# Turning three of four feature chunks by transposing transfers instead of TensorE

## The chip, the cores and the metric

The kernel runs on one core of one Trainium2 chip. The metric is the time of one execution in device microseconds (us), taken as the median of several runs. The engines named below are TensorE (PE: matrix products, with its weight loads listed as PEld), VectorE (DVE), ScalarE (ACT), GpSimd (POOL) and SyncE (SP), whose queue issues nearly all transfers of this kernel (SPq in the profile).

## The reference

The input x has 2048 rows (tokens) of 640 features. The output is x plus an attention block and an MLP block, both of which see x after two layer norms in a row (one outside, one within the MLP, or one for the attention).

```
xn = layernorm(x)
q, k, v = split(xn @ wqkv)                 # 32 heads of 20 features
o = softmax(q k^T / sqrt(20)) v            # per head, over all 2048 tokens
A = concat(o) @ wo
h = gelu(layernorm(xn) @ w1 + b1)          # 640 -> 1536
B = h @ w2 + b2                            # 1536 -> 640
out = x + A + B
```

The products are needed at about single precision. The kernel gets there with 16-bit operands: each number is written as a sum of a high and a low float16, and a product of two such sums is taken as three TensorE passes (high by high, high by low, low by high).

## The kernel before, in words

The kernel has two stages. The first, up to about 232 us, makes q, k and v of all tokens and prepares the weights of the MLP. The second holds the attention, with the MLP's products and the last projection woven between its scores; the change does not touch it. In the first stage a manual schedule is in force: each engine executes its instructions in the order in which the program text issues them, and the same holds for the queue of SP. A wait at the head of an engine's list holds up all that stands behind it.

The tokens are taken in four chunks c = 0 to 3 of 512. For each chunk, `load_x` (L169) brings four tiles `xt` of 128 rows by 640 features, of which five buffers exist. `norm_a`, `norm_b` and `norm_c` (L230 to L252) compute the layer norms on VectorE, scale the tiles in place, and store 512 numbers of 4 bytes each to `rscr` (L252). TensorE needs the features on the partitions. So `transp` (L262) turns the 20 blocks of 128x128 of a chunk on TensorE with an identity, in three groups of 8, 8 and 4 blocks, into PSUM, and `transp_out` copies them from there, with ScalarE for the high half (L269) and VectorE for the low half (L270), into the tile `xnt` of the chunk. After the last group the whole tile is also stored to `xscr` (L272) for the MLP.

The products of a chunk follow. `qk(c, tt)` for tt = 0 to 4 (L286) makes a pair of 128 columns of q or k for the 512 tokens, thirty products of 128x512. `qk_out` evicts it: ScalarE writes the high half (L300), VectorE the low half (L301), the squares for the heads' lengths follow (L304 on ScalarE in chunk 0, L306 on VectorE after it), and SP stores both halves to `qkscr` (L308, 256 KB each). `lengths()` (L321) is a small TensorE product on those squares; it stands after the next `qk` in TensorE's order, so TensorE waits there if the squares are late. Then `vproj(c, j)` for j = 0 to 3 (L349) makes the values and `vproj_out` evicts them (L359, L361). All these products, and before the change the turned blocks, share three buffers of PSUM (pool `psS`).

While chunk c is multiplied, chunk c + 1 is normalized and turned: its `transp` groups stand after tt = 2, 3 and 4 of chunk c. The x tiles of chunk c + 2 are requested after tt = 4.

Beside this runs the preparation of weights. In chunk 0 the weights of k and v are split (L382, L383), w2 (L474) and w1 (L482) are requested by SP, 3.8 MB each, and the generator `weights()` then yields slices of work which `some(n)` places: sums of squares of w2 (L415, six slices), a scale, sums of squares of w1 (L423, five slices), a scale, common factors, and the splitting of w2 and w1 into halves (L125 to L127). These run on ScalarE and VectorE between the evictions.

The row of constants is `brow`, 32 heads by 2048 float16. GpSimd fills it at the start (L446), the row of ones for k is stored to `bscr` (L458), and in the last chunk `shifts()` scales it per head (L340) and stores it (L341), from where the first scores' operands read it.

The instructions issued by SP wait, each, for the transfer issued eight before it, since eight semaphores are used in turn.

Of the kernel before, what the change touches and what calls it, by code (L numbers as in the profile page):

```python
# [8 lines left out]
F16 = mybir.dt.float16  # L9
BF16 = mybir.dt.bfloat16  # L10
I32 = mybir.dt.int32
AF = mybir.ActivationFunctionType
# [4 lines left out]
P = 128  # L17
S, D, H, DH, F = 2048, 640, 32, 20, 1536
KD = D // P
# [23 lines left out]
def mha_mlp_kernel(tc, x, wqkv, wo, w1, b1, w2, b2, out):  # L43
    nc = tc.nc
# [3 lines left out]
    with (  # L48
# [9 lines left out]
        xscr = dram.tile([P, KD, 2, S], F16, name="xscr")  # L58
# [6 lines left out]
        bscr = dram.tile([H + 1, S], F16, name="bscr")  # L65
# [12 lines left out]
        w1t = keep.tile([P, KD, F], F32, name="w1t")  # L78
# [76 lines left out]
        with tc.tile_pool(name="pa", bufs=2) as pa, tc.tile_pool(name="pa1", bufs=1) as pa1, tc.manual_schedule():  # L155
# [7 lines left out]
            xts = {}  # L163
# [31 lines left out]
            for m in range(KD):  # L195
# [3 lines left out]
                nc.gpsimd.affine_select(heads[:, m, :], heads[:, m, :], pattern=[[DH, H]],  # L199
                                        compare_op=ALU.is_ge, fill=0.0, base=DH - 1 - m * P,  # L200
                                        channel_multiplier=-1)
            brow = pa1.tile([H, S], F16, name="brow")
            lmx = pa1.tile([P, 2, 4], F32, name="lmx")

            def warm(n):
# [48 lines left out]
            xnts = {}  # L254

            def transp(c, k0, pts):
                if k0 == 0:
                    xnts[c] = pa.tile([P, KD, 2, 512], F16, tag="xnt", name=f"xnt{c}")
                pt = psS.tile([P, 2, 512], F32, tag="s", name="pt")
                for j in range(4):  # L260
                    for k in range(min(2, KD - k0)):
                        nc.tensor.transpose(pt[:, k, j * P : (j + 1) * P],  # L262
                                            xts[c][j][:, (k0 + k) * P : (k0 + k + 1) * P], ident)
                pts.append((c, k0, pt))

            def transp_out(c, k0, pt):
                nk = min(2, KD - k0)
                ks = slice(k0, k0 + nk)
                nc.scalar.activation(xnts[c][:, ks, 0, :], pt[:, :nk], AF.Copy)  # L269
                nc.vector.tensor_sub(xnts[c][:, ks, 1, :], pt[:, :nk], xnts[c][:, ks, 0, :])  # L270
                if k0 + 2 > KD:
                    nc.sync.dma_start(xscr[:, :, :, c * 512 : (c + 1) * 512], xnts[c])  # L272
                    del xts[c]

            PASS = ((0, 0), (0, 1), (1, 0))

            def qk(c, tt):
                ps = psS.tile([P, 2, 512], F32, tag="s", name="qkp")
                order = [(i, k) for i in range(2) for k in range(KD)]
                if c + tt == 0:  # L280

                    order = [(i, k) for k in range(KD) for i in range(2)]
                for i, k in order:
                    q, mm = divmod(2 * tt + i, KD)
                    for n, (a, b) in enumerate(PASS):
                        nc.tensor.matmul(ps[:, i, :], wv[:, k, q, a, mm * P : (mm + 1) * P],  # L286
                                         xnts[c][:, k, b, :], start=(k + n == 0), stop=(k == KD - 1 and n == 2))
                return ps
# [39 lines left out]
            def shifts():  # L328

                b = sm.tile([H, 2], F32, tag="b", name="b")  # L330
                bq = sm.tile([H, 2, 4], F32, tag="bq", name="bq")
                for r in range(4):
                    nc.vector.tensor_reduce(bq[:, :, r], lmx[32 * r : 32 * r + 32], AX.X, ALU.max)
                nc.vector.tensor_reduce(b, bq, AX.X, ALU.max)
                nc.vector.tensor_scalar(b[:, 0:1], b[:, 0:1], b[:, 1:2], 1e-30, ALU.mult, ALU.max)
                nc.gpsimd.tensor_tensor(b[:, 0:1], b[:, 0:1], half, ALU.pow)
                nc.vector.tensor_scalar(b[:, 0:1], b[:, 0:1], -1.01, TOP / QS, ALU.mult, ALU.add)
                nc.vector.tensor_scalar(b[:, 0:1], b[:, 0:1], 0.0, -65504.0 * KROW, ALU.min, ALU.max)
                nc.vector.tensor_scalar(b[:, 0:1], b[:, 0:1], 1.0 / KROW, 1.0 / KROW, ALU.mult, ALU.mult)
                nc.vector.tensor_scalar(brow, brow, b[:, 0:1], None, ALU.mult)  # L340
                nc.sync.dma_start(bscr[:H, :], brow)  # L341

            def vproj(c, j):
                ps = psS.tile([P, 2, 512], F32, tag="s", name="vp")
                for hf in range(2):
                    n = 0
                    for k in range(KD):
                        for a, b in PASS:
                            nc.tensor.matmul(ps[:, hf, :320], xnts[c][:, k, a, j * P : (j + 1) * P],  # L349
# [18 lines left out]
            def sums(tag, ws):  # L368
                accs[tag] = squares(ws, junk)
# [9 lines left out]
            def split_qkv(n):  # L379
                q = "qkv".index(n)  # L380
                for k in range(KD):
                    nc.scalar.activation(wv[:, k, q, 0], stage[n][:, k], AF.Copy, scale=scales[n])  # L382
                    nc.vector.scalar_tensor_tensor(wv[:, k, q, 1], stage[n][:, k], scales[n], wv[:, k, q, 0],  # L383
                                                   ALU.mult, ALU.subtract)
# [54 lines left out]
            def some(n):  # L439
                for _ in range(n):  # L440
                    next(slices, None)
# [7 lines left out]
            pts = []  # L449
# [5 lines left out]
            for t in pts:  # L455
                transp_out(*t)
            split_qkv("q")
            nc.sync.dma_start(bscr[H : H + 1, :], brow[0:1, :])  # L458
            nc.sync.dma_start(b1t, b1.rearrange("(k p) -> p k", p=P))
            for c in range(4):  # L460
                nxt = c + 1 if c < 3 else None
                for tt in range(5):
                    ps = qk(c, tt)
                    lengths()

                    if c == 0:
                        if tt == 0:
                            sums("k", [stage["k"][:, 0:3], stage["k"][:, 3:]])
                            norm_c(0)
                            scale_of("k")  # L470
                        elif tt == 1:
                            split_qkv("k")
                            norm_a(1)
                            nc.sync.dma_start(w2t, w2.rearrange("(k p) n -> p k n", p=P))  # L474
                        elif tt == 2:
                            sums("v", [stage["v"][:, 0:3], stage["v"][:, 3:]])
                            norm_b(1)
                            scale_of("v")
                        elif tt == 3:
                            norm_c(1)  # L480
                            split_qkv("v")
                            nc.sync.dma_start(w1t, w1.rearrange("(k p) n -> p k n", p=P))  # L482
                    else:
                        if nxt and tt < 3:
                            (norm_a, norm_b, norm_c)[tt](nxt)
                            some(1)
                        else:
                            some(2)
                    qk_out(c, tt, ps)
                    if nxt and tt >= 2:  # L490
                        pts = []
                        transp(nxt, 2 * (tt - 2), pts)
                        transp_out(*pts[0])
                if c + 2 < 4:
                    load_x(c + 2)
                if c == 3:
                    stack = load_stack(0, 0)
                    for _ in range(6):
                        next(stack)
                for j in range(4):  # L500
                    ps = vproj(c, j)
                    lengths()
                    if j == 0 and c == 3:
                        shifts()
                        for _ in stack:
                            pass
                    some(2 if c < 3 else 1)
                    vproj_out(c, j, ps)
            some(99)

# [1 line left out]
        with ExitStack() as scope:  # L512
# [47 lines left out]
            def project(ot, acc, t0, j):  # L560
                for hf in range(2):
# [3 lines left out]
                    for k in range(KD):  # L565
                        for a, b in PASS:
                            nc.tensor.matmul(ps[:, :320], ot[:, k, a, j * P : (j + 1) * P], wov[:, k, b, cols],
# [209 lines left out]
            def layer1(mc, f):  # L777
# [4 lines left out]
                for i in range(2):  # L782
                    n = 0
                    fo_ = (f + i) % 4 * P
                    for k in range(KD):
                        for a, b in PASS:
                            nc.tensor.matmul(ps[:, i], w1v[:, k, (f + i) // 4, a, fo_ : fo_ + P], xnt[:, k, b, :],  # L787
# [23 lines left out]
            def layer2(mc, j, hf):  # L811
# [5 lines left out]
                for f in range(KF):  # L817
                    for a, b in PASS:
                        nc.tensor.matmul(ps[:, :320], hTs[mc][:, f, a, j * P : (j + 1) * P],  # L819
# [52 lines left out]
            def projection():  # L872
                known = lambda c: ready[2 * c // NMC] == len(UNITS)
                for c in range(NMC):
# [9 lines left out]
                    for j in range(MC // P):  # L884
                        after = ended[0]
                        for h in range(2):
# [7 lines left out]
                            for k in range(KD):  # L894
                                for a, b in PASS:
                                    nc.tensor.matmul(ps[:, :320], ot[:, k, a, j * P : (j + 1) * P],  # L896
# [30 lines left out]
            with tc.manual_schedule():  # L927
# [5 lines left out]
                for g, hf, cc, kb0 in groups:  # L933
# [26 lines left out]
                    if cc == 0 and kb0 == 0 and (g, hf) != ORDER[-1]:  # L960
                        n = ORDER[ORDER.index((g, hf)) + 1]
                        sides.append(load_stack(*n, *([stacks[g, hf][1]] if n[0] == g else [])))
                n = 0
# [119 lines left out]
```

## Time and profile before

| | us |
|---|---|
| median of three runs | 1384.39 |
| the three runs | 1383.70, 1384.39, 1385.21 |
| the profiled execution's own time | 1385.2 |
| its span, first to last instruction | 1383.5 |
| first stage, to the first score | 0 to 232.5 |

The profile shows one execution. A row of its lists of instructions gives the start and the length in us, the engine, the line, the operation, its output and inputs with their shapes, how many instructions were merged, and in brackets the idle time before it and what ended that. Rows of SPq are the issuing of transfers, not their landing; the length of such a row holds the waits between the merged issues. In a table by stretches each engine has its busy time in us with the count of instructions in parentheses; then follow the granted clock of TensorE, the busy share of the DMA engines and the rate in GB/s. TensorE's clock is 0.997 of full speed over the span.

### The profile page before, as it was taken

To read this page: it belongs to the slowest core of one execution; us is meant where nothing else is said; L and a number is where in the kernel's file an instruction comes from. 1 tells how busy PE (TensorE), PEld (TensorE's weight loads), DVE (VectorE), ACT (ScalarE), POOL (GpSimd) and SP (SyncE) were. 2 spreads that over 40 slices of the span, in tenths; PEclk is the share of its full clock that TensorE was granted. 3 is DMA by queue.
4 is the path that set the end of the run, shared out by engine and by line. 5 is a ranking of instruction groups with operands and counts; after the bars stand their busy time and mean duration, and the time that the engine had idled before them with its cause. 6 is when DMAs were issued, how large, how long until landed. Compare 5 with 4: busy or idle time off the path is not lost.

```text
span 1383.5 us, 29113 instructions
## 1 busy us (share of the span) xinstructions
PE 1350.8 (98%) x11711; PEld 600.9 (43%) x11711; DVE 1061.7 (77%) x1425; ACT 1126.2 (81%) x1282; POOL 32.9 (2%) x75
## 2 busy tenths in 40 slices
PE   9999999999999999999999999999999999999998
PEld 6555555443333343433343333343334334333375
DVE  6648743899778977889887789877988897888642
ACT  5644323999999999999999999999999999999700
POOL 2000000000000000000000000000000000000000
PEclk9999999999999999999999999999999999999999
DMA  9853413012124231213221123212124322341375
GB/s 265 243 175 109 108 52 110 16 32 64 41 55 111 67 88 34 69 52 102 71 77 33 47 75 103 76 47 58 44 64 113 98 56 70 85 153 59 98 235 179
DMA packets 92320, 125.68 MB, mean 91 GB/s; under 512 B 16905, under 2 KB 58569, under 8 KB 92178
## 3 DMA queue, kind: packets, MB, share of 16 engines
q1 hardware_dynamic: 89218, 117.14, 28.3%
q0 software_dynamic: 2304, 5.24, 2.3%
q8 instruction: 94, 1.54, 0.5%
q10 hardware_dynamic: 656, 1.36, 0.3%
q14 instruction: 48, 0.39, 0.1%
HBM read 80.84 MB, written 42.86 MB: 89 GB/s over the span
## 4 chain that ended last, share of the span: by engine, by line
PE 59%; DVE 11%; ACT 5%; DMA 3%; issue 2%; SPq 1%; DVEq 0%; ACTq 0%
PE o L615 23%; PE s L584 14%; PE py L819 9%; PE pu L787 8%; DVE low L598 5%; PE z L896 5%; ACT p L586 4%; DMA oscr<-oa 1%; DVE u L740 1%; DMA oa<-opart 1%; DVE u L741 1%; DVE w L744 1%; DVE w L745 1%; DVE hT L752 1%; DVE u L750 1%
## 5 line engine op out<-in xcount | busy, mean ns | idle before, releaser
L586 ACT ACTIVATE p<-s 128x1024 f32<-128x1024 f32 x1024 | 973.6, 1042 | 52.4 <-PE s L584 46.2
L598 DVE TENSOR_TENSOR low<-p 128x1024 f16<-128x1024 f32 x512 | 608.8, 1219 | 165.0 <-ACT p L586 164.9
L615 PE MATMUL o<-p,vfull 128*32 128x512 bf16 (+1 forms) x4096 | 433.7, 494 | 0.0
L584 PE MATMUL s<-qs,ks 61*128 61x512 f16 x2048 | 317.7, 382 | 8.7 <-ACT p L586 7.2
L584 PEld LDWEIGHTS <-ks 61*128 61x128 f16 x2048 | 63.9, 94 | 296.4 <-issue 294.2
L787 PE MATMUL pu<-xm,w1t 128*128 128x256 f16 x1440 | 179.2, 274 | 4.1 <-DVE u L740 3.6
L819 PE MATMUL py<-w2t,hT 128*128 128x320 f16 x1152 | 178.6, 301 | 1.7 <-DVE xb L757 1.7
L787 PEld LDWEIGHTS <-w1t 128*128 128x128 f16 x1440 | 130.9, 98 | 71.2 <-issue 57.6
L819 PEld LDWEIGHTS <-hT 128*128 128x128 f16 x1152 | 102.5, 98 | 89.5 <-issue 55.2
L286 PE MATMUL qkp<-xnt,wv 128*128 128x512 f16 x600 | 132.3, 380 | 0.0
L615 PEld LDWEIGHTS <-vfull 128*32 128x32 f16 x3072 | 61.5, 95 | 146.2 <-issue 115.4
L615 PE MATMUL o<-low,vfull 128*32 128x512 f16 x1024 | 107.3, 379 | 6.6 <-DVE low L598 6.4
L300 ACT ACTIVATE qkhl<-qkp,qks 128x1024 f16<-128x1024 f32 (+1 forms) x24 | 23.3, 971 | 84.1 <-PE qkp L286 66.2
L286 PEld LDWEIGHTS <-wv 128*128 128x128 f16 x600 | 58.2, 98 | 67.8
L615 PEld LDWEIGHTS o<-p,vfull 128*32 128x32 f32 x2048 | 63.1, 109 | 50.6 <-issue 0.5
L349 PE MATMUL vp<-wv,xnt 128*128 128x320 f16 x480 | 66.6, 300 | 0.0
L896 PE MATMUL z<-w1t,ot 128*128 128x320 f16 x480 | 65.8, 300 | 0.0
L896 PEld LDWEIGHTS <-ot 128*128 128x128 f16 x480 | 46.7, 98 | 19.8 <-issue 1.7
L349 PEld LDWEIGHTS <-xnt 128*128 128x128 f16 x480 | 46.5, 98 | 18.2
L301 DVE SCALAR_TENSOR_TENSOR qkhl<-qkp,qks,qkhl 128x1024 f16<-128x1024 f32 (+1 forms) x24 | 26.5, 1104 | 34.3 <-ACT qkhl L300 34.3
L857 DVE SCALAR_TENSOR_TENSOR acc<-z,sc,acc 128x320 f32<-128x320 f32 x32 | 17.6, 550 | 45.1 <-PE z L896 42.9
L636 ACT ACTIVATE ev<-o 128x512 f32<-128x512 f32 x64 | 39.4, 615 | 3.3 <-PE o L615 3.3
(168 smaller groups left out, 685.7 us busy)
## 6 DMA issues: line engine op xcount, KB each, us to landing
qkscr<-qkhl SPq DMA_DIRECT2D x40, 256.0 KB
opart<-ev SPq DMA_DIRECT2D x124, 80.0 KB
ks<-qkscr SPq DMA_DIRECT2D x120, 80.0 KB
qs<-qkscr SPq DMA_DIRECT2D x192, 40.0 KB
oa<-opart SPq DMA_DIRECT2D x32, 240.0 KB
xt<-in_A_x_dram SPq DMA_DIRECT2D x16, 320.0 KB
xscr<-xnt SPq DMA_DIRECT2D x4, 1280.0 KB
xm<-xscr SPq DMA_DIRECT2D x8, 640.0 KB
```

Of the source, the lines that this page charges most:

```text
L286: nc.tensor.matmul(ps[:, i, :], wv[:, k, q, a, mm * P : (mm + 1) * P], xnts[c][:, k, b, :], start=(k + n == 0), stop=(k == KD - 1 and n == 2))
L300: nc.scalar.activation(hl[:, 0, i0:i1], ps[:, i0:i1], AF.Copy, scale=a)
L301: nc.vector.scalar_tensor_tensor(hl[:, 1, i0:i1], ps[:, i0:i1], a, hl[:, 0, i0:i1], ALU.mult, ALU.subtract)
L349: nc.tensor.matmul(ps[:, hf, :320], xnts[c][:, k, a, j * P : (j + 1) * P], wv[:, k, 2, b, hf * 320 : (hf + 1) * 320], start=(n == 0), stop ...
L584: nc.tensor.matmul(ps[:, a, :], ks[64 * a : 64 * a + 61, kb * P : (kb + 1) * P], qs[64 * a : 64 * a + 61, cc * 512 : (cc + 1) * 512], star ...
L586: nc.scalar.activation(pt, ps, AF.Exp, scale=QS)
L598: nc.vector.tensor_sub(low, pt, upper(pt))
L615: nc.tensor.matmul(pv.o[32 * q : 32 * q + 32, :], src[:, v0 - PAD * (1 - q % 2) :][:, :32], t, start=q not in pv.begun, stop=last, skip_gr ...
L636: nc.scalar.activation(evs[g, hf][:, cc], pv.o, AF.Copy)
L787: nc.tensor.matmul(ps[:, i], w1v[:, k, (f + i) // 4, a, fo_ : fo_ + P], xnt[:, k, b, :], start=(n == 0), stop=(n == 3 * KD - 1))
L819: nc.tensor.matmul(ps[:, :320], hTs[mc][:, f, a, j * P : (j + 1) * P], w2v[:, f, b, hf * 320 : (hf + 1) * 320], start=(n == 0), stop=(n == ...
L896: nc.tensor.matmul(ps[:, :320], ot[:, k, a, j * P : (j + 1) * P], wov[:, k, b, h * 320 : (h + 1) * 320], start=(n == 0), stop=(n == 3 * KD ...
```

## The change

The first chunk is turned as before. For the chunks 1 to 3 a new function `turn(c, j)` handles one tile of 128 rows: ScalarE and VectorE write its high and low halves, still with the tokens on the partitions, into a tile `row` (128 by 1280 float16, two buffers), and SP issues a transposing transfer from `row` into the columns of `xnt` that belong to these rows. There are twelve of these transfers of 320 KB. The tile j = 0 stands after tt = 2, j = 1 and 2 after tt = 3, j = 3 after tt = 4; the store to `xscr` follows the last one and waits for all four.

With it, the request for w1 moves in SP's order: it stood in chunk 0 ahead of the fourth pair's stores, and now stands after the store of `xscr` of chunk 1, still ahead of the request for the x tiles of chunk 2. One slice fewer of the weights' preparation is placed in the last value product of chunk 0, so the first sum of squares of w1 moves into chunk 1. `brow` has 512 instead of 2048 columns, and the two stores of it read it four times over.

```diff
-            brow = pa1.tile([H, S], F16, name="brow")
+            brow = pa1.tile([H, S // 4], F16, name="brow")
...
+            def turn(c, j):
+
+                if j == 0:
+                    xnts[c] = pa.tile([P, KD, 2, 512], F16, tag="xnt", name=f"xnt{c}")
+                xv = xts[c][j].rearrange("p (k n) -> p k n", k=KD)
+                row = pa.tile([P, KD, 2, P], F16, tag="row", name="row")
+                nc.scalar.activation(row[:, :, 0, :], xv, AF.Copy)
+                nc.vector.tensor_sub(row[:, :, 1, :], xv, row[:, :, 0, :])
+                nc.sync.dma_start(xnts[c].rearrange("p k s t -> p (k s) t")[:, :, j * P : (j + 1) * P],
+                                  row.rearrange("p k s n -> p (k s n)"), transpose=True)
+                if j == 3:
+                    nc.sync.dma_start(xscr[:, :, :, c * 512 : (c + 1) * 512], xnts[c])
+                    del xts[c]
...
-                nc.sync.dma_start(bscr[:H, :], brow)
+                nc.sync.dma_start(bscr[:H, :].rearrange("h (r t) -> h r t", r=4), brow[:, None, :].to_broadcast([H, 4, S // 4]))
...
-            nc.sync.dma_start(bscr[H : H + 1, :], brow[0:1, :])
+            nc.sync.dma_start(bscr[H : H + 1, :].rearrange("h (r t) -> h r t", r=4), brow[0:1, None, :].to_broadcast([1, 4, S // 4]))
...
                             norm_c(1)
                             split_qkv("v")
-                            nc.sync.dma_start(w1t, w1.rearrange("(k p) n -> p k n", p=P))
...
                     if nxt and tt >= 2:
-                        pts = []
-                        transp(nxt, 2 * (tt - 2), pts)
-                        transp_out(*pts[0])
+                        for j in ((0,), (1, 2), (3,))[tt - 2]:
+                            turn(nxt, j)
+                    if c == 0 and tt == 4:
+                        nc.sync.dma_start(w1t, w1.rearrange("(k p) n -> p k n", p=P))
...
-                    some(2 if c < 3 else 1)
+                    some(1 if (c, j) == (0, 3) or c == 3 else 2)
```

## Prediction

> **What bounds the kernel now.** I read the busy shares first, then the chain of work that ended last, then the busy time in four stretches of the first stage (core, stretch, its length, then busy time and count of each engine, granted clock, DMA share, GB/s).
>
> ```profile
> PE 1350.8 (98%) x11711; PEld 600.9 (43%) x11711; DVE 1061.7 (77%) x1425; ACT 1126.2 (81%) x1282; POOL 32.9 (2%) x75
> PE 59%; DVE 11%; ACT 5%; DMA 3%; issue 2%; SPq 1%; DVEq 0%; ACTq 0%
> 76.00:130.00 54.00, 53.51 (x337) 29.56 (x336) 37.89 (x97) 24.37 (x33) 2.01 (x2) 1.00 0.41 132
> 130.00:182.00 52.00, 52.00 (x328) 28.58 (x327) 37.99 (x76) 20.36 (x28) 2.36 (x2) 1.00 0.31 77
> ```
>
> TensorE is busy 98% of the span. In the two middle chunks it is busy 53.51 of 54 and 52.00 of 52 us, VectorE 38, ScalarE 20 to 24. So a TensorE instruction that goes is time won, until something else becomes late. The attention stage, from 232 us on, is untouched; whatever is won or lost is settled before it. The stage's cadence is in TensorE's list in order of time (start, us, engine, line):
>
> ```profile
> 41.37 0.38 PE L110 MATMUL mxp<-acc,ones 128*128 128x2 f32 x2
> 42.15 1.91 PE L262 MATMUL pt<-ident,xt 128*128 128x128 f32 x8 [0.39 <-DVE xt L243]
> 43.96 6.63 PE L286 MATMUL qkp<-xnt,wv 128*128 128x512 f16 x30
> ...
> 50.75 1.09 PE L262 MATMUL pt<-ident,xt 128*128 128x128 f32 x8
> 51.68 6.64 PE L286 MATMUL qkp<-xnt,wv 128*128 128x512 f16 x30
> ...
> 58.47 0.66 PE L262 MATMUL pt<-ident,xt 128*128 128x128 f32 x4
> 58.97 4.24 PE L349 MATMUL vp<-wv,xnt 128*128 128x320 f16 x30
> ...
> 75.74 13.11 PE L286 MATMUL qkp<-xnt,wv 128*128 128x512 f16 x60
> 88.78 0.30 PE L321 MATMUL norms<-sq,heads 128*32 128x128 bf16 x8
> 89.01 6.65 PE L286 MATMUL qkp<-xnt,wv 128*128 128x512 f16 x30
> ...
> 129.39 13.11 PE L286 MATMUL qkp<-xnt,wv 128*128 128x512 f16 x60
> ...
> 182.04 13.11 PE L286 MATMUL qkp<-xnt,wv 128*128 128x512 f16 x60
> ...
> 232.47 0.61 PE L584 MATMUL s<-qs,ks 61*128 61x512 f16 x4
> ```
>
> **Removed from TensorE.** In the first chunk the turning holds TensorE from 41.75 to 43.96, 50.75 to 51.68 and 58.47 to 58.97: 2.2 + 0.9 + 0.5 = 3.6 us. The chunk from 129.39 to 182.04 takes 52.65 us with twenty turns, the last one, to 232.47, takes 50.43 without: 2.2 us. The chunk from 75.74 has the same twenty: 2.2 us. At most 3.6 + 2.2 + 2.2 = **8.0 us** go.
>
> **Swapped on ScalarE and VectorE.** Per chunk three copies from PSUM become four row copies of 128x640. Nearest rows, the splitting of w2:
>
> ```profile
> L125 ACT ACTIVATE wtmp<-w2t,s 128x640 f32<-128x640 f32 x12 | 9.8, 823 | 4.3 <-DVE w2t L127 4.2
> L127 DVE TENSOR_TENSOR w2t<-wtmp,w2t 128x640 f16<-128x640 f32 x12 | 9.9, 826 | 0.4
> ```
>
> Four cost 3.3 us on each engine, under 1 us more than now. In the middle chunks TensorE hides it (above). The shorter row of constants shortens one VectorE instruction in the last chunk and cuts its store into 128 pieces instead of 32; the scores start only when the last value product ends (232.47), so I take nothing.
>
> **Added: twelve transposing transfers T0 to T3** of 320 KB, chunk by chunk, on SP's queue. No row shows one. Call its time on the rings t. From below: 320 KB at the 409 GB/s of the w1 load (quoted next) is 0.8 us. From above: the 512 four-byte pieces of the rscr store keep the rings from full speed for some 9.5 us (next paragraph), 19 ns a piece; a turn that wrote pieces of 32 bytes (a choice of mine) would make 10,240 of them, 190 us. The ends are far apart; the nearest row by size is the bulk load, and because the pieces are shorter I take nearly twice that, t = 1.4 us plus 0.5 us to land. The Trainium skill (DMA: Bandwidth & Descriptors, Latency and other measured facts) gives 261 GB/s for a DMA transpose with a non-contiguous middle dimension, as here; t would be 1.25 us, an estimate from that page, and the sum below 0.6 us lower; no row here shows it.
>
> **What the transfers queue behind.** SP's list, the DMA rate in four stretches, and ScalarE's list:
>
> ```profile
> 51.80 0.37 SPq L252 DMA_DIRECT2D rscr<-r  x1
> 55.78 0.38 SPq L482 DMA_DIRECT2D w1t<-in_B_w_dram  x1
> 56.26 8.67 SPq L308 DMA_DIRECT2D qkscr<-qkhl  x4
> 65.02 4.48 SPq L272 DMA_DIRECT2D xscr<-xnt  x1
> 69.59 7.25 SPq L169 DMA_DIRECT2D xt<-in_A_x_dram  x4
> ```
>
> ```profile
> 53.00:62.50 9.50, 9.50 (x64) 5.37 (x63) 6.10 (x7) 5.21 (x6) 0.00 (x0) 1.00 0.50 56
> 62.50:71.00 8.50, 8.50 (x71) 5.93 (x69) 2.81 (x5) 8.41 (x15) 0.00 (x0) 1.00 1.00 409
> 71.00:77.50 6.50, 6.50 (x47) 4.30 (x45) 0.93 (x6) 5.00 (x7) 0.00 (x0) 1.00 1.08 383
> 77.50:81.00 3.50, 3.50 (x18) 1.61 (x17) 1.02 (x4) 0.47 (x2) 0.00 (x0) 1.00 0.89 339
> ```
>
> ```profile
> 62.44 0.58 ACT L269 ACTIVATE xnt<-pt 128x512 f16<-128x512 f32 x1
> 62.92 1.26 ACT L415 ACTIVATE junk<-w2t 128x1280 bf16<-128x1280 f32 x1
> ...
> 72.04 0.69 ACT L359 ACTIVATE vfull<-vp 128x640 f32<-128x640 f32 x1
> ```
>
> After rscr (2 KB in 4-byte pieces, issued 51.80) the rings move 56 GB/s for 9.5 us, though w1t's 3.8 MB wait from 55.78 on; then 409. In the changed order SP issues T0, rscr, the stores of the fourth pair of columns, T1, T2, the fifth pair's stores, T3, xscr, w1t, the next x. T0 sits ahead of rscr, so the slow time ends at 62.5 + 1.4, about 64. T1 stands behind rscr and two 256 KB stores: on the rings until 66.1, landed 66.6.
>
> There are only two row buffers, so ScalarE's third row copy waits for T0 and the fourth for T1: the **added wait**. Behind the fourth stand, on ScalarE, the squares of w2 and the value products' evictions, which free the product buffers that TensorE needs. In before those take from 62.92 to 72.73; after a copy begun at 66.6 they end at 77.1, and TensorE starts chunk 1 there, not at 75.74 - 3.6 = 72.1. The 3.6 us are lost here, and 1.4 more.
>
> T2 ends at 67.5, the fifth pair's stores at 68.9, T3 at 70.3, landed 70.8. Only then come xscr (3.4 us), w1t (9.6 us at 409 GB/s), x (3.4 us): 87.2 instead of 81, **6.2 us late**. VectorE waits for that x ahead of its half of chunk 1's first eviction:
>
> ```profile
> 79.94 0.89 DVE L230 BATCH_NORM_STATS2 st<-xt 128x6 f32<-128x320 f32 x2 [2.92 <-DMA xt<-in_A_x_dram]
> ...
> 84.17 1.28 DVE L301 SCALAR_TENSOR_TENSOR qkhl<-qkp,qks,qkhl 128x1024 f16<-128x1024 f32 x1
> 85.37 0.68 DVE L306 TENSOR_TENSOR sq<-qkhl 128x1024 bf16<-128x1024 f16 x1
> ```
>
> The squares end at 86.05 now, at 92.2 then. TensorE needs them for the norms product after its first two column pairs: 77.1 + 13.1 = 90.2 against 88.78 now. It waits to 92.2: 3.4 us later than before. The moved w1 square on ScalarE waits for w1t to 83.8 and its eviction ends near 87, under that.
>
> In the two later chunks T3 is issued about four us after the last column pair (eviction, squares, row copy) and the next chunk's products begin 17 us after that pair (58.97 to 75.74); four T at 1.4 us with ten stores at 0.7 and xscr and x at 3.4 each are 19 us of ring in 50 us. Hidden, and SP's issue time, unseen, would have to exceed 3 us a transfer to matter. There 2.2 + 2.2 = 4.4 us stay won.
>
> **Sum:** +3.4 - 4.4 = -1.0 us. The profiled execution took 1385.2 us around a span of 1383.5; the median of three is 1384.39, 0.8 lower, inside their spread of 1.5. On the median: **1383.4 us**. Each us on t adds four to the x chain, so t from 0.8 to 2.0 us gives -3.4 to +1.4: 1381.0 to 1385.8.
>
> **Rivals.**
> *Past the slow time (faster).* rscr's pieces and the stores go to memory outside the core, T does not; if the slow time is memory's, T1 lands early, the fourth copy waits for nothing and chunk 1 starts at 72.1. The x chain then is late only by T0, 1.4 us: squares at 87.5, before needed at 85.2, so 1.3 us earlier than before. -1.3 - 4.4 = -5.7: 1378.7 us. Against it: the stores stand ahead of T1 in one queue, and w1t's load, which writes into the core, crawled as well.
>
> *Slow rings (slower).* The same chain with t above 2.0 us, from which the four T in the first chunk take back more than the later chunks win. At t = 5: 1383.4 + 4 x 3.6 = 1397.8 us. Later chunks still hide it up to t near 9. For it: the short pieces of a turn; against: the bulk rate.
>
> *Block after block (slower).* If a transfer's ten 128x128 blocks follow one another at 1.4 us each, t = 14: the first chunk loses 4 x 12.6 = 50, the next two are ring-bound at 56 + 13.4 = 69 against 50 us, 19 each: 1383.4 + 88 = 1471 us. The Trainium skill (VectorE: DVE Perf Modes, The three transpose paths) speaks for this: it gives 1309 ns for one 128x128 block by DMA against 390 ns by TensorE; ten of the first make t = 13.1, an estimate from that page, and 1383.4 + 82 = 1465 us. The trace has TensorE's side lower still (20 turns in 2.2 us, with pipelining); nothing here shows the other.
>
> *Not what it says.* Chunk 0 is still turned by TensorE; the order of instructions has the sixty later ones gone, so I give this none.
>
> **How the numbers follow.** Forecast 0.37, past the slow time 0.25, slow rings 0.33, block after block 0.05. A measurement of this kernel can tell about 0.2%, 2.8 us, from no change. Faster: 0.25 + 0.07 of the forecast (t under 0.95) = 0.32. Same: 0.30 of the forecast + 0.04 of the slow rings (t under 2.3) = 0.34. Slower: 0.29 + 0.05 = 0.34. The range runs from 1377 (a little under the faster rival) to 1398 (slow rings at t = 5); slow rings beyond that (0.10) and blocks (0.05) are left out. The forecast's own range is 1381.0 to 1385.8.
>
> **What would show it.** Right: no L262 after 21 us; the fourth row copy waiting on a transfer to 65-68 us; the first BATCH_NORM_STATS2 after 84 us with a DMA named; TensorE idle before norms near 90; 50.4 us from the third chunk's first product to the fourth's. Wrong: that copy at 60 (faster rival); T landing over 2.5 us apart (slow rings); TensorE idle before the third or fourth chunk's first product (blocks).

## The result, and the profile after

The changed kernel takes 1389.56 us (median of 8 runs, 1388.64 to 1395.46), the kernel before beside it 1385.51 (8 runs, 1383.70 to 1388.35): a ratio of 1.0035, with a 95% interval of 1.0026 to 1.0044. It is slower by 0.35%, some 4.9 us, where 1.0 us less was forecast; the time lies inside the range of 1377 to 1398. The profiled execution took 1389.7 us around a span of 1387.8, against 1385.2 around 1383.5 before. The readings below split these 4.3 us of span.

First TensorE's list in order of time after the change (start, us, engine, line, in brackets the idle time before the row and what ended it), to be laid beside the list of before in the prediction:

```profile
19.66 6.22 PE L300 MATMUL qkp<-xnt,wv 128*128 128x512 f16 x28 [0.42 <-DVE wv L397]
...
73.06 6.88 PE L363 MATMUL vp<-wv,xnt 128*128 128x320 f16 x30 [5.48 <-DVE vfull L375]
...
79.92 13.11 PE L300 MATMUL qkp<-xnt,wv 128*128 128x512 f16 x60
97.71 0.41 PE L335 MATMUL norms<-sq,heads 128*32 128x128 bf16 x8 [4.68 <-DVE sq L320]
98.05 8.76 PE L300 MATMUL qkp<-xnt,wv 128*128 128x512 f16 x30
...
139.04 13.11 PE L300 MATMUL qkp<-xnt,wv 128*128 128x512 f16 x60
189.38 13.11 PE L300 MATMUL qkp<-xnt,wv 128*128 128x512 f16 x60
...
239.81 0.61 PE L598 MATMUL s<-qs,ks 61*128 61x512 f16 x4
```

The turning is gone (no L262 from here on), but TensorE stands idle twice for over 4 us, 5.48 us before the first chunk's fourth value product and 4.68 us before the second chunk's norms. Each time what follows takes longer than the same thing elsewhere: 6.88 us instead of 4.24 (58.97 before) for thirty value products, 8.76 instead of 6.65 (89.01 before) for thirty q and k products. The table by stretches (TensorE's busy time first, its granted clock third from the end) says why:

```profile
71.60:78.40 6.80, 5.34 (x21) 3.05 (x22) 1.65 (x2) 6.74 (x11) 0.00 (x0) 0.50 0.76 208
...
95.50:102.30 6.80, 4.59 (x19) 1.63 (x19) 6.53 (x17) 1.78 (x3) 2.00 (x2) 0.50 0.23 77
```

Each time the granted clock is half for 6.8 us, a stretch that begins within the idle time. The two groups of products take 2.64 + 2.11 = 4.7 us longer by it, and the prediction has no term for that. Only the 2.11 us lengthen the whole: the 2.64 lie ahead of the wait for x, which would have been longer without them (e3 shows this below). What the two idle times wait for is seen on ScalarE, on VectorE and in SP's list:

```profile
68.17 0.74 ACT L281 ACTIVATE row<-xt 128x640 f16<-128x640 f32 x1 [10.26 <-DMA xnt<-row]
...
90.77 1.48 ACT L437 ACTIVATE junk<-w1t 128x1536 bf16<-128x1536 f32 x1 [10.08 <-DMA w1t<-in_B_w_dram]
```

```profile
91.54 0.89 DVE L230 BATCH_NORM_STATS2 st<-xt 128x6 f32<-128x320 f32 x2 [10.34 <-DMA xt<-in_A_x_dram]
...
96.98 0.68 DVE L320 TENSOR_TENSOR sq<-qkhl 128x1024 bf16<-128x1024 f16 x1
```

```profile
46.97 5.07 SPq L283 DMA_TRANSPOSE xnt<-row  x1
52.13 0.53 SPq L252 DMA_DIRECT2D rscr<-r  x1
...
56.08 10.88 SPq L283 DMA_TRANSPOSE xnt<-row  x2
...
69.79 1.34 SPq L283 DMA_TRANSPOSE xnt<-row  x1
73.16 0.60 SPq L286 DMA_DIRECT2D xscr<-xnt  x1
73.81 0.78 SPq L507 DMA_DIRECT2D w1t<-in_B_w_dram  x1
74.69 3.81 SPq L169 DMA_DIRECT2D xt<-in_A_x_dram  x4
```

The fourth row copy waits for a transposing transfer until 68.17 (10.26 us), with the evictions of the value products behind it in ScalarE's order. The third chunk's x arrives for VectorE at 91.54, where it was 79.94 before. Both waits are the ones named in the prediction; both end later than it said. While the fourth row copy waits, the rings move 46 GB/s, behind the store to `rscr`:

```profile
56.00:67.20 11.20, 11.20 (x90) 7.87 (x89) 2.08 (x3) 1.88 (x2) 0.00 (x0) 1.00 0.87 46
```

Where the 4.3 us of span come from, by the two lists of TensorE: the first long run of products begins 1.50 us earlier (19.66 against 21.16; two single products stand ahead of it, from 18.65); from there to the second chunk 60.26 us instead of 54.58, +5.68 (a third wait, of 1.48 us at 54.62, is part of it); from there to that chunk's norms 17.79 instead of 13.04, +4.75; half clock behind them +2.11; the rest of that chunk -1.39; the third chunk 50.34 instead of 52.65, -2.31; the fourth 50.43 as before; and from the first score to the end of the span 1148.0 instead of 1151.0, -3.0. Together +4.3.

### The profile page after: what moved, and what is told of

The parts are those of the page before. It is cut to its first block, busy times and chain, and to the rows that moved or that the text cites. A ratio compares the mean times of both kernels' runs of the same rounds, so it can differ in the third digit from the quotient of the medians.

```text
span 1387.8 us, 29026 instructions
## 1 busy us (share of the span) xinstructions
PE 1344.7 (97%) x11651; PEld 593.8 (43%) x11651; DVE 1060.2 (76%) x1428; ACT 1126.4 (81%) x1285; POOL 31.7 (2%) x75
## 3 DMA queue, kind: packets, MB, share of 16 engines
q10 hardware_dynamic: 656, 1.36, 0.3%
## 4 chain that ended last, share of the span: by engine, by line
PE 61%; DVE 11%; ACT 4%; DMA 2%; issue 2%; SPq 1%; DVEq 0%; ACTq 0%
PE o L629 23%; PE s L598 15%; PE py L833 10%; PE pu L801 8%; PE z L910 5%; DVE low L612 5%; ACT p L600 4%; DVE u L754 1%; DMA oa<-opart 1%; DVE u L755 1%; DMA oscr<-oa 1%; DVE w L758 1%; DVE hT L766 1%; DVE w L759 1%; DVE u L764 1%
## 5 line engine op out<-in xcount | busy, mean ns | idle before, releaser
L363 PE MATMUL vp<-wv,xnt 128*128 128x320 f16 x480 | 69.4, 306 | 5.5 <-DVE vfull L375 5.5
```

## The experiments

The theory (A): two delays of queue order eat the gain. One is the slow time of the rings behind the store to `rscr`, with T1 to T3 behind it; the other is that the next x stands behind T3, the store to `xscr` and w1t. Against it stood that one delay alone is the cost, that the half clock is, that the transfers' own time is, or the shorter row. Each ratio is to the kernel before, run on the same chip. The 2 by 2 table of the two delays comes first, since the later runs fill it:

| | x behind `xscr` and w1t | x first |
|---|---|---|
| `rscr` where the change leaves it | the change: 1.0035 | e5: 0.998 |
| `rscr` moved away | e10: 0.996 | e8: 0.9919 |

**e1, the store to `rscr` of the second to fourth chunks behind the request for the next x.**

```diff
-                nc.sync.dma_start(rscr[c * 512 : (c + 1) * 512].rearrange("(j p) -> p j", p=P), r2)
+                late[c] = r2
+                if c == 0:
+                    store_r(c)
...
                 if c + 2 < 4:
                     load_x(c + 2)
+                if nxt:
+                    store_r(nxt)
```

> The changed kernel with one thing moved: the store of 512 four-byte numbers (rscr) of chunks 1 to 3 is issued behind the request for the next x tiles, not between the turning transfers. Theory A (the slow time after that store holds up T1, and with it the fourth row copy, the value products and the x chain): the fourth row copy begins near 59 us instead of 68.2, no TensorE idle before the fourth value product of chunk 0, the next x lands near 80 instead of 91.5, no idle before the norms product of chunk 1, TensorE's granted clock 0.997 again; time 11 to 13 us under the changed kernel, about 1377 us against 1385.5 before. Theory B (the transfers are slow by themselves: 1.3 us of issue and 1.9 us of ring each, whatever stands ahead): the copy still begins after 64 us, the time falls by less than 4 us, 1386 or more.

Measured: 1387.45 us, ratio 1.001 (0.9995 to 1.0026). TensorE, then VectorE:

```profile
69.76 13.11 PE L307 MATMUL qkp<-xnt,wv 128*128 128x512 f16 x60
92.59 0.41 PE L342 MATMUL norms<-sq,heads 128*32 128x128 bf16 x8 [9.72 <-DVE sq L327]
```

```profile
82.57 0.89 DVE L230 BATCH_NORM_STATS2 st<-xt 128x6 f32<-128x320 f32 x2 [11.52 <-DMA xt<-in_A_x_dram]
...
89.40 0.89 DVE L230 BATCH_NORM_STATS2 st<-xt 128x6 f32<-128x320 f32 x2 [3.72 <-DMA xt<-in_A_x_dram]
```

The first idle time is gone whole, and the second chunk begins at 69.76 instead of 79.92. But TensorE then waits 9.72 us for the norms' squares: x is still late, its fourth tile until 89.40, with the slow store now right behind it. The first half of A held; the time did not follow (1377 was expected), because the second delay was left, and made worse: with x in the same place and the store elsewhere, e10 below has these norms at 87.53.

**e2, three row buffers.**

```diff
-                row = pa.tile([P, KD, 2, P], F16, tag="row", name="row")
+                row = pa.tile([P, KD, 2, P], F16, tag="row", name="row", bufs=3)
...
-                sq = pa.tile([P, 2, 512], BF16, tag="sq", name="sq", bufs=2)
+                sq = pa.tile([P, 2, 512], BF16, tag="sq", name="sq", bufs=1)
```

> The changed kernel with three row buffers instead of two (room made by one buffer instead of two for the squares). The fourth row copy then waits for T0, not T1. Theory A: the copy begins near 58 us, ScalarE and the value products of chunk 0 go on, TensorE reaches chunk 1 near 73 instead of 79.9; but T3 still lands behind the slow time, x comes 2 to 3 us earlier at best, so TensorE waits some 8 us before the norms product instead of 4.7 and drops its clock once instead of twice: 2 to 4 us under the changed kernel, 1386 to 1388. Theory B': the first stall is the whole cost: 7 us under the changed kernel, 1382.

Measured: 1390.68 us, ratio 1.0029 (1.001 to 1.0047), as the change itself. ScalarE's fourth row copy no longer waits:

```profile
58.87 0.72 ACT L281 ACTIVATE row<-xt 128x640 f16<-128x640 f32 x1
```

```profile
74.00 13.12 PE L300 MATMUL qkp<-xnt,wv 128*128 128x512 f16 x60 [0.47 <-DMA xnt<-row]
98.46 0.41 PE L335 MATMUL norms<-sq,heads 128*32 128x128 bf16 x8 [11.34 <-DVE sq L320]
```

```profile
92.29 0.89 DVE L230 BATCH_NORM_STATS2 st<-xt 128x6 f32<-128x320 f32 x2 [17.63 <-DMA xt<-in_A_x_dram]
```

The second chunk begins 5.9 us earlier than with two buffers, and all of it is spent waiting before the norms. The added wait on ScalarE is real but costs nothing while x is late: the transfers themselves are late behind `rscr`, so x is too. Both expected times, 1386 to 1388 and 1382, were missed. More buffers do not mend a late queue.

**e3, TensorE kept busy in the first idle time**, with 18 added products whose output is not used, between the third and the fourth value product (36 in the profile, 4.18 us).

```diff
+                    if (c, j) == (0, 2):
+                        for _ in range(18):
+                            nc.tensor.matmul(ps[:, 0, 320:448], ones, ones, start=True, stop=True)
```

> The changed kernel with 18 idle products of 128x128 (no use of their result) on TensorE ahead of the fourth value product of chunk 0, where it now stands idle for 5.5 us. They end before the wait does. If the half clock after the stall comes from standing idle: the fourth value product takes 4.2 us instead of 6.9 and the time falls by 2 to 3 us, to about 1387, though the wait itself stays. If the product is slow because the transfers and ScalarE work beside it: it stays at 6.9 us and the time at 1389.6.

Measured: 1391.87 us, ratio 1.0043 (1.0026 to 1.006).

```profile
55.63 0.29 PE L335 MATMUL norms<-sq,heads 128*32 128x128 bf16 x8 [2.62 <-ACT sq L318]
55.86 5.92 PE L363 MATMUL vp<-wv,xnt 128*128 128x320 f16 x30
...
74.65 4.25 PE L363 MATMUL vp<-wv,xnt 128*128 128x320 f16 x30 [0.36 <-DVE vfull L375]
...
80.25 13.11 PE L300 MATMUL qkp<-xnt,wv 128*128 128x512 f16 x60 [0.20 <-ACT vfull L373]
99.30 0.41 PE L335 MATMUL norms<-sq,heads 128*32 128x128 bf16 x8 [5.94 <-DVE sq L320]
```

The fourth value product is back at 4.25 us: the half clock comes from standing idle. In this execution the fourth row copy itself comes later (69.75 instead of 68.17). From it to the second chunk 10.50 us pass instead of 11.75, so 1.25 us are won there. They are lost again in the wait for x: from the issue of T3 (71.37 here, 69.79 in the change) to the second chunk's norms 27.9 us pass in both. The time expected, 1387, did not come. In this run 2.62 us of idle time at 55.63 was already followed by a slow product, 5.92 for 4.25.

**e5, x first: the request for the third chunk's x right behind T3, then w1t, then the store to `xscr`.**

```diff
                 if j == 3:
-                    nc.sync.dma_start(xscr[:, :, :, c * 512 : (c + 1) * 512], xnts[c])
+                    if c > 1:
+                        nc.sync.dma_start(xscr[:, :, :, c * 512 : (c + 1) * 512], xnts[c])
...
-                    if c == 0 and tt == 4:
-                        nc.sync.dma_start(w1t, w1.rearrange("(k p) n -> p k n", p=P))
                 if c + 2 < 4:
                     load_x(c + 2)
+                if c == 0:
+                    nc.sync.dma_start(w1t, w1.rearrange("(k p) n -> p k n", p=P))
+                    nc.sync.dma_start(xscr[:, :, :, 512:1024], xnts[1])
```

> The third chunk's x is asked for right behind the second chunk's last transposing transfer, then w1t, and the second chunk's store to xscr last. Theory A (x behind xscr and w1t sets the end): x lands about 12 us earlier, the first BN_STATS2 of the third chunk at 79 to 82 us (91.5 in the changed kernel), TensorE's idle of 4.68 us before the second chunk's norms and the 2.1 us of half clock behind it go, the idle of 5.48 us before the first chunk's fourth value product stays: 6.8 us less than the changed kernel, 1382 to 1384. Rival (the squares of w1 on ScalarE wait for w1t, now behind x, and hold the evictions instead): idle of 3 us or more in the second chunk with ScalarE named, within 2 us of the changed kernel.

Measured: 1383.65 us, ratio 0.998 (0.9963 to 0.9997).

```profile
74.02 6.70 PE L364 MATMUL vp<-wv,xnt 128*128 128x320 f16 x30 [4.05 <-DVE vfull L376]
80.70 13.11 PE L301 MATMUL qkp<-xnt,wv 128*128 128x512 f16 x60
94.04 0.29 PE L336 MATMUL norms<-sq,heads 128*32 128x128 bf16 x8 [0.23 <-DVE sq L321]
...
233.91 0.61 PE L600 MATMUL s<-qs,ks 61*128 61x512 f16 x4
```

Moving three issues in SP's list takes the second idle time and its half clock away and brings the scores 5.9 us forward (239.81 to 233.91). The first idle time stays, as A has it. The rival's wait exists, ScalarE stands 8 us for w1t, but TensorE loses only 0.23 us by it.

**e6, transposing transfers for the third and fourth chunks only; the second is turned by TensorE, with w1t asked for where it was before.**

```diff
-                    if nxt and tt >= 2:
+                    if c == 0 and tt >= 2:
+                        pts = []
+                        transp(nxt, 2 * (tt - 2), pts)
+                        transp_out(*pts[0])
+                    elif nxt and tt >= 2:
```

> The second chunk is turned by TensorE again and w1t is asked for where it was before; the third and fourth chunks go by transfers, the short row stays. Theory A (all that the change loses is lost beside the second chunk's turn; later transfers are hidden): start 1.5, 2.2 and 2.2 us of TensorE's time, and up to 3 us at the second stage's start less than before: 1377 to 1381, no idle over 1 us in the second or third chunk. Rival (transfers cost wherever they stand, through the slow rings behind the store of rscr): idle of 2 us or more with a transfer named in the second or third chunk, 1384 or more.

Measured: 1377.84 us, ratio 0.9942 (0.992 to 0.9963); no idle time over 1 us on TensorE in the second or third chunk. All that the change loses is lost beside the second chunk's turn. Behind later chunks the same transfers, with the same slow store in their midst, are hidden. Since e6 puts the request for w1t back as well, it does not tell the turn from the place of w1t.

**e7, e5 and the stores to `rscr` of the second to fourth chunks issued a chunk later.**

```diff
                     qk_out(c, tt, ps)
+                    if c > 0 and tt == 0:
+                        store_r(c)
```

> As e5, and the store to rscr of the second to fourth chunks is issued a chunk later, behind the first q and k product of its own chunk, so that neither the transposing transfers nor x go beside it. Theory A (two delays, both of queue order: T1 behind rscr, x behind xscr and w1t): neither idle is left, no half clock before the scores, the second chunk begins near 69 us, and the ledger comes out at its gains alone, 1.5 + 3.6 + 2.2 + 2.2 + 3.0 = 12.5 us less than before: 1373 to 1377. Rival (the transfers' own issue and ring time, 3.3 us each, are what makes x late): x still lands after the squares are wanted, idle of over 3 us before the second chunk's norms, 1380 or more.

Measured: 1377.1 us, ratio 0.9934 (0.9909 to 0.9959), just above what A gave, and below the rival's. TensorE, then ScalarE:

```profile
55.62 0.29 PE L343 MATMUL norms<-sq,heads 128*32 128x128 bf16 x8 [3.15 <-ACT sq L326]
55.85 4.25 PE L371 MATMUL vp<-wv,xnt 128*128 128x320 f16 x30
...
72.64 13.11 PE L308 MATMUL qkp<-xnt,wv 128*128 128x512 f16 x60
```

```profile
53.37 1.11 ACT L322 ACTIVATE qkhl<-qkp,qks 128x1024 f16<-128x1024 f32 x1 [4.05 <-DMA qkscr<-qkhl]
```

Both idle times are gone. What is late next stands in the first row: 3.15 us, because ScalarE's eviction before it waits 4.05 us for an older store to `qkscr` to free its rows. The first chunk's own store to `rscr`, which e7 leaves, stands ahead of those stores; e8 tries whether it is the cause.

**e8, as e7, with the first chunk's store to `rscr` moved to the second chunk as well.**

```diff
-                if c == 0:
-                    store_r(c)
...
                     if c > 0 and tt == 0:
-                        store_r(c)
+                        store_r(c if c > 1 else 0)
...
                     vproj_out(c, j, ps)
+                    if (c, j) == (1, 0):
+                        store_r(1)
```

> As e7, and the first chunk's store to rscr leaves the first chunk too: it is issued behind the second chunk's first q and k product, the second chunk's store behind that chunk's first value product. Theory A (the store to rscr holds the q and k stores, the q and k rows have few buffers, so ScalarE's eviction waits 4.05 us for qkscr at 53 us and TensorE 3.15 us for the norms' squares): both waits go, the second chunk begins 3 us earlier than in e7 (72.64), and the time is 1372.5 to 1375.5. Rival (w1t, which then lands earlier or later, or the two stores in the second chunk, hold that chunk's products instead): idle of 3 us or more in the second chunk, no less than 1376.

Measured: 1373.94 us (5 runs, 1372.47 to 1374.09), ratio 0.9919 (0.9905 to 0.9934): 11.2 us less than before, and the fastest version here.

```profile
69.79 13.11 PE L306 MATMUL qkp<-xnt,wv 128*128 128x512 f16 x60
83.68 0.29 PE L341 MATMUL norms<-sq,heads 128*32 128x128 bf16 x8 [0.77 <-DVE sq L326]
...
223.54 0.60 PE L609 MATMUL s<-qs,ks 61*128 61x512 f16 x4
```

The first chunk now runs without a gap. Up to that wait the first chunk's store is the only one that stands elsewhere than in e7, and ScalarE's wait for `qkscr` at this eviction is in every trace that keeps it (1.12 us in e1, 1.38 before, 2.69 in the change, up to 4.16 in e5) and in none of the three that move it (e8, e10, e11): the store is the cause. But its price differs from execution to execution: e1 keeps it and begins the second chunk at 69.76, as e8 does. So the 2.9 us by which e8's second chunk begins ahead of e7's are not the price of this store in general, and the intervals of their two ratios overlap. The transfers are as many and as large as in the change.

**e10, the stores to `rscr` moved as in e8, x left behind `xscr` and w1t as in the change.** The edit is e8's without that of e5.

> The changed kernel with all stores to rscr moved as in e8, and the order of xscr, w1t and x left as in the change. Theory A (two separate delays): the fourth row copy and the second chunk's start are those of e8 (58 and 70 us), but x stands behind xscr and w1t, its first BN_STATS2 comes near 82.5 us as in e1, TensorE waits some 6 us for the second chunk's norms with 2 us of half clock behind it: 7 to 8 us more than e8, 1381 to 1383. Rival (once rscr is out of the way the order of x no longer matters): within 2 us of e8, 1374 to 1376, no idle over 2 us in the second chunk.

Measured: 1379.84 us, ratio 0.996 (0.9946 to 0.9973), between the two expectations and nearer to A's.

```profile
87.53 0.40 PE L340 MATMUL norms<-sq,heads 128*32 128x128 bf16 x8 [4.56 <-DVE sq L325]
87.86 8.17 PE L305 MATMUL qkp<-xnt,wv 128*128 128x512 f16 x30
...
229.42 0.60 PE L607 MATMUL s<-qs,ks 61*128 61x512 f16 x4
```

The order of x is worth 229.42 - 223.54 = 5.9 us here, as it was with `rscr` in the way (e5). The place of `rscr` is worth 239.81 - 229.42 = 10.4 us. The two are separate and add up: 1.0035 - 0.9919 is 1.16%, 16 us.

**e11, the kernel before with nothing but its stores to `rscr` moved as in e8.**

> The kernel before with nothing but the stores to rscr moved as in e8. Theory A (the store only costs what stands behind it and is waited for; in the kernel before TensorE is busy 39.41 of 40 us in the first chunk): within 1 us of before, 1384 to 1386. Rival (e8 is faster because of the moved stores, not of the transposing transfers): 4 us or more less than before, 1381 or less.

Measured: 1385.6 us, ratio 0.9995 (0.9984 to 1.0005): no difference. The moved stores are not what makes e8 fast; in the kernel before nothing that TensorE needs stands behind them.

**e4 and e9, the kernel before with the shorter row of constants alone**, the same kernel twice.

> The kernel before with only the shorter row of constants. In the changed kernel the first product started 1.5 us earlier, and one small VectorE instruction (L217) beside GpSimd's filling of that row took 0.17 instead of 1.36 us. Theory: filling a row a quarter as long is out of the way of VectorE, the first product starts near 19.5 instead of 21.2, and the time is 1 to 1.8 us under before. Rival: the earlier start is chance of that one profile (x landing): time as before within 0.5 us.

> The kernel before with the shorter row of constants alone, once more, since the first time did not resolve it: its trace began the first product 2.27 us earlier than before and the scores 2.69 us earlier, its time was level with before. If the trace is typical: 2 to 3 us less than before, ratio 0.998. If the earlier start is chance of the two profiled runs: ratio 1.000, and this run's first product begins near 21 us.

Measured: ratios 0.9998 (0.9982 to 1.0013) and 0.9994 (0.9984 to 1.0004). In the traces VectorE's small step L217 at the start takes 1.36 us before, beside GpSimd's fill of the row, and 0.17 us with the shorter fill:

```profile
10.38 1.79 POOL L446 MEMSET brow<- 32x2048 f16 x1
```

```profile
10.85 1.36 DVE L217 TENSOR_SCALAR at<-at 128x4 f32<-128x4 f32 x1
```

Both rows are the kernel before; in e4 the fill takes 0.52 us and the step 0.17. The first full run of products begins at 18.89 (e4) and 19.70 (e9), against 21.16 before, but in e9 0.52 + 0.62 us come back as idle time in the first chunk, and its span is nearly that of before, 1383.7. Part of the earlier start is chance: e11, with the long fill, begins that run at 20.34. Whatever is left, up to 0.2%, the times do not resolve.

## Why the prediction was wrong, point by point

**TensorE's 8.0 us**, given as the most that could go, were right in kind and nearly in size. The third chunk takes 50.34 us from its first product to the next chunk's, as forecast (2.3 us less), in the change and in e8 alike. In e8 the first chunk, from its second pair of columns (25.57) to the second chunk, takes 44.22 us instead of 47.97, 3.75 less where 3.6 were forecast; but the second chunk takes 52.99 instead of 53.65, 0.7 less and not 2.2, since TensorE still waits 0.77 and 1.11 us there.

**The copies and the second half of the change** were right: no long wait of TensorE comes from the copies, and e6 shows the later chunks' transfers hidden.

**The added wait** was right in place, kind and nearly in size: until 68.17 instead of 66.6 us. By its own terms T1 would have been on the rings until 66.8, not 66.1 (64, two stores at 0.7, then 1.4), and 0.7 of the 1.6 us are this slip. The second chunk begins at 79.92 instead of 77.1: 1.6 us from that, and 1.25 from the half clock, by which 11.75 us pass from the copy to the second chunk where 10.5 were forecast and e3 has 10.50.

**The x chain is the step that failed**, "T3 at 70.3, landed 70.8", then "xscr (3.4 us), w1t (9.6 us at 409 GB/s), x (3.4 us)", squares at 92.2. The mechanism is as described; its terms were too small, and they come in a row. On the rings the transfer was nearly as assumed. This stretch of the trace of after holds T3 on the rings, the next the pause behind it, the third the store to `xscr`:

```profile
71.00:72.60 1.60, 0.00 (x0) 0.00 (x0) 0.42 (x1) 1.60 (x4) 0.00 (x0) 0.70 1.09 201
```

```profile
72.50:74.50 2.00, 1.44 (x6) 0.87 (x7) 0.51 (x1) 1.97 (x3) 0.00 (x0) 0.50 0.08 20
74.50:79.50 5.00, 5.00 (x24) 2.99 (x23) 0.83 (x1) 4.08 (x8) 0.00 (x0) 0.60 1.01 290
```

1.6 us at 201 GB/s is 322 KB: t is 1.6 us, not 1.4. (The Trainium skill, DMA: Bandwidth & Descriptors, Latency and other measured facts, has 261 GB/s for it; 201 here.) But the transfer occupies SP for 1.34 us before its first packet moves, and from T3's issue to the store that waits for it 73.16 - 69.79 = 3.37 us pass, where 1.9 were taken. Then the rings stand nearly empty for almost two us, until the store's own packets come; and the store takes nearly five us at 290 GB/s, where 3.4 were taken from a stretch at 383. So w1t is there at 90.77 instead of 83.8, x right behind it, and the squares end at 97.66 instead of 92.2: 5.5 us late on the forecast, 0.7 of them by the slip named above. The forecast of -1.0 us, plus these 5.5, plus 2.1 of half clock behind them, plus 0.7 by which the rest of the second and third chunk gained less than 4.4 (1.39 + 2.31), less 3.0 in the second stage (below), makes the measured +4.3. The slope given, "Each us on t adds four to the x chain", was put on the time on the rings, while the issue and the pause, which it left out, are as long.

**A term that was missing** is the half clock: 2.11 us of the time, behind the wait for x, besides the 2.64 us that this wait hides. The prediction let TensorE wait as if a wait cost its own length. The Trainium skill (TensorE: Matmul & The Clock Gate, Part 1: The HAM clock gate) says that the clock falls to half after an idle window of about 3.4 us and rises after a busy one, and that the windows are free-running, so that they do not start with the kernel's own work. The runs bear this out in the main: the half clock lasted one, two or three times 3.4 us, namely 3.4 in e3 (2.62 us idle) and e10 (4.56), 6.8 twice in the change (5.48 and 4.68) and 10.2 in e1 and e2 (9.72 and 11.34). But 2.62 us idle in e3 were enough, and 2.80 in e2 and 3.15 in e7 were not followed by it, so the length of a wait alone does not settle it.

**The shorter row taken as nothing** stands within what the times resolve.

**The second stage, taken as untouched**, gained 3.0 us. Before, the MLP's first input is asked for only when the first stage's last product ends, and TensorE waits for it; after, ahead of the scores. SP and TensorE of before, then SP of after:

```profile
232.57 0.59 SPq L773 DMA_DIRECT2D xm<-xscr  x1
```

```profile
237.01 0.82 PE L787 MATMUL pu<-xm,w1t 128*128 128x256 f16 x6 [0.54 <-DMA xm<-xscr]
```

```profile
234.91 0.59 SPq L787 DMA_DIRECT2D xm<-xscr  x1
```

This holds in every version with transposing transfers: span less first score is 1148.0 (after), 1148.5 (e5), 1148.3 (e6) and 1148.6 (e8), against 1151.0 (before), 1151.7 (e9) and 1153.1 (e11, first score at 231.23). TensorE's wait of 0.54 us is only the start of it. Some 5 us into the stage TensorE of before goes at half clock for 3.4 us, and TensorE of after does not; the first row is before, the second after, both 5.3 us behind the first score:

```profile
237.80:241.20 3.40, 3.40 (x25) 0.85 (x24) 2.36 (x2) 2.81 (x4) 0.00 (x0) 0.50 0.96 274
```

```profile
245.10:248.50 3.40, 3.25 (x33) 1.35 (x33) 2.36 (x2) 3.40 (x5) 0.00 (x0) 1.00 0.15 41
```

The traces of e4, e9 and e11 have this half clock too, those of e6, e7 and e8 do not. By the ninth softmax tile on ScalarE (L586, at 241.98 before) 1.6 of the 3.0 us are won, in e5, e6 and e8 as well; the rest comes in small steps from 448 us on, and its cause is open. Why the input can be asked for earlier was not tried by itself.

**The rivals.** "Slow rings" named the right kind and the wrong cause: later chunks hide the transfers, the first does not, but not because t is large. That the time lies inside the range is therefore luck in part: above 1385.8 the range stood for t over 2.0, and t was 1.6. "Past the slow time" was refuted in the change, where T1 waits until the slow time ends. What it had foreseen, a fourth copy that does not wait for it and an early second chunk, came only in e1, e8 and e10, where the store stands elsewhere. "Block after block" did not occur; its second sum, for t = 13.1, comes to some 78 us by its own steps, not 82.

## What to carry to other kernels

A transfer that replaces work of a busy engine takes its place in a queue, and what it costs is the place: here the change was worth +4.9 us or -11.2 us with the same transfers, by where a 2 KB store in 4-byte pieces and one request for input stood beside them. That it is the small pieces which make this store slow is likely from its size, but no run stores the same numbers in larger ones. In a chain of dependent transfers count for each the issue, the time on the rings and the way to the one that waits (here 1.34 + 1.6 + some 0.5 us), and the pause before the next one's packets. And price a wait of a matrix engine of over some 3 us at more than its length, since a time at half clock can follow it (1.5 to 2.6 us here, in e10 and the change).

## What the runs showed of the hardware that was not expected

- A transposing transfer of 320 KB within the core took 1.34 us of its issuing queue and 1.6 us on the rings (201 GB/s).
- TensorE's granted clock was 0.5 for 3.4 us around an idle time of 4.56 us (e10), for 6.8 us around 4.68 and 5.48 us (the change), and for 10.2 us around 9.72 and 11.34 us (e1, e2). In the kernel before it was 0.5 for 3.4 us, from 237.8 us on, without an idle time of more than 0.54 us in the 5 us ahead of it.
- In e2 the fourth tile's row was written by 60.5 us (ScalarE's half from 58.87), and SP still issued its transfer only at 70.0, the last of the four in this line of e2 (shortest, median and longest issue in ns, then the first and the last start in us): the queue in which it stood held it, not the buffer.

```profile
L283 SPq DMA_TRANSPOSE xnt<-row x4: 1476/4368/8337, 47.4 to 70.0; - x4
```

- A fill of 32x2048 by GpSimd (1.79 us) stretched one VectorE step of 128x4 elements from 0.17 to 1.36 us while both ran.
